# The start of a fused causal-convolution and GELU-MLP kernel: block 0's tokens in order, block 1's x issued earlier, W_in chunks in another order, and taps of the convolution joined

## The chip, the cores and the metric

The kernel runs on one core of a Trainium2 chip. The core has five engines with separate instruction streams: PE (TensorE, matrix products into PSUM), DVE (VectorE), ACT (ScalarE), POOL (GpSimd) and SP (SyncE, which here only issues DMAs). They meet at semaphores. ACT and POOL issue some DMAs too, and all DMAs are carried out by the same 16 DMA engines. The metric is the device time of one execution in microseconds (us), as the median over runs; smaller is better.

## The reference, cut to what matters

x has 8 sequences of 4096 tokens with 192 features; 8 heads of 24 features share 7 convolution weights each. The weights go through a softmax over the taps, the convolution is causal along the sequence, and its result goes through a two-layer MLP with exact GELU.

```python
w = np.exp(weight - np.max(weight, axis=-1, keepdims=True))
w = w / (np.sum(w, axis=-1, keepdims=True) + 1e-09)            # [8 heads, 7 taps]
x_pad = np.concatenate([np.zeros((B, 6, D)), x], axis=1)
idx = np.arange(S)[:, None] + np.arange(7)[None, :]
x_unf = x_pad[:, idx, :].reshape(B, S, 7, 8, 24)
conv = np.einsum('hk,bskhg->bshg', w, x_unf).reshape(B * S, 192)
h = conv @ w_in                                                # [32768, 2048]
g = 0.5 * h * (1.0 + erf(h / sqrt(2)))
out = g @ w_out                                                # [32768, 192]
```

## The kernel before, in words

**Layout.** The 32768 tokens are cut into two halves of 16384. A block takes the same stretch of tokens from both halves: the first six blocks (0 to 5) have 256 tokens of each half, the others 512. Half 0 lies in partitions 0 to 63 and half 1 in partitions 64 to 127. The 192 features are three planes (p = 0, 1, 2) of 64, feature 3j+p in plane p, row j of a half.

**Load (`load`, L319).** x of a block comes in four DMAs, one for each half and each half of the features (q), in fp32, 32 tokens side by side in the partitions, into one of three buffers `xin`. For block 0 each partition takes eight neighbouring tokens in one piece of 1440 floats (5760 bytes, of which the other feature half is not used); for the other blocks each token's half row is a piece of its own, 96 floats (384 bytes). So block 0's tokens sit in another order than those of the other blocks, and its halo, its taps' offsets (32 columns per tap) and its stores follow that order.

**Convolution.** DVE transposes `xin` into `xT` (`trans`, L518; three calls, one for each plane). For blocks 0 and 1 the convolution is done by PE: the planes are cast to bf16 into `xTb` (ACT for block 0, POOL for block 1), PE multiplies by seven diagonal matrices `dg` (`pconv`, L700) into the four PSUM banks `ob`, and ACT and DVE copy the result to `xc` (`conv_out`, L182). For blocks from 2 on DVE does it (`conv`, L538): for each tap k and each plane p one call, the first a multiplication (L555), the other six a multiply-add onto `acc` (L562), the last of them writing `xc` in bf16. For blocks 4, 5 and 6 ACT does tap 0 (`first_tap`, L652). POOL copies the six columns of halo between blocks (`halo`, L408).

**The two products.** `mm1` (L737) multiplies `xc` by `win` into `hp`, two buffers of two banks; one slice i holds two chunks of 128 hidden features for a block of 256 tokens and one chunk for a block of 512. ACT does the GELU from `hp` into `gT` (L684). `mm2` (L793) and for the long blocks `mm2_t` (L823) multiply by `wout` into `ob`. The product with W_out of block n-1 is cut into units that are put between the slices of block n, so PE's order is written out by hand: slice, units, slice, units. DVE and ACT bring `ob` to `osb`, and SP stores it.

**W_in and W_out.** W_in comes by three pairs of POOL DMAs (pieces of 256, 256 and 512 columns); each half of the partitions loads only its own 1024 columns, and DVE copies each piece across to the other half (`dup`, L501). `CH` (L87) is the order in which a half uses its 16 chunks. W_out comes in fp32 by four SP DMAs and POOL casts it (`S_WOG` counts the casts).

**Order at the start.** Each engine runs its list in order. SP: weights, half of block 0's x, a wait for the first piece of W_in (L873), block 1's x, four DMAs of W_out, x of blocks 2 and 3, and then loads and stores in turn. DVE: softmax, the diagonals `dg`, `trans(0)`, two `conv_out` of block 0, `dup(0)`, `dup(1)`, `trans(1)`, `dup(2)`, `conv_out` of block 1, block 2. PE: 16 matmuls on zeros (L698), `pconv` of block 0, slices of block 0, with `pconv` of block 1 behind slices 4 and 5 (`behind`, L732), and so on. A slice waits until the GELU two slices before has emptied its `hp` buffer.

Of the kernel before, what the change touches and what calls it, by code (L numbers as in the profile page):

```python
# [11 lines left out]
def bass_lightweight_conv__then__act_gelu_exact_kernel(  # L12
# [36 lines left out]
    HX = 8  # L49
# [3 lines left out]
    HL = 32 * HB  # L53
    XB = HL + WS[0]
# [32 lines left out]
    CH = [[(8 * hf + i) % NF for i in range(NF)] for hf in range(2)]  # L87
# [3 lines left out]
    for n in range(NB):  # L91
        k = 64 if n == 0 or M0 <= n < M1 else 16 * NG[n] if n < NB - 1 else 32 * NG[n]
        OUTS.append(k * (NG[0] if n == 0 else 1) + (OUTS[n - 2] if n >= 2 else 0))
# [15 lines left out]
    with es:  # L109
# [94 lines left out]
        NCV = NP * KS  # L204
# [6 lines left out]
        def cast(e, n, p):  # L211
            e.wait_ge(S_TR, NP * n + p + 1)
            e.tensor_copy(
                ap(xTb[PC[n]], p * XB + HX, [[NP * XB, 128], [1, WS[n]]]),
                ap(xT[n % 2], p * XW + HX, [[NP * XW, 128], [1, WS[n]]]),
            ).then_inc(S_CAST[PC[n]])

        def cvd(n):

            return sum(NCV - NP * (m in K0) for m in range(n + 1) if m not in PC)  # L220


        HC = [0]
        for n in range(NB):
            HC.append(HC[n] + (1 + NP if n == 0 else 1))
# [93 lines left out]
        def load(e, n, qs=(0, 2, 1, 3), sm=None):  # L319
            mb = WS[n] // 32  # L320
            if n >= NX:
                e.wait_ge(S_TR, NP * (n - NX + 1))
            for q in qs:
                off = ((q // 2) * HALF + OFF[n]) * D + DQ * (q % 2)
                if n == 0:

                    dst = [[TB // 32 * DQ, 32], [1, mb * D - DQ]]
                    src = [[mb * D, 32], [1, mb * D - DQ]]
                else:
                    dst = [[TB // 32 * DQ, 32], [DQ, mb], [1, DQ]]  # L330
                    src = [[D, 32], [32 * D, mb], [1, DQ]]
                e.dma_start(  # L332
                    ap(xin[n % NX], 32 * q * (TB // 32 * DQ), dst), ap(xt, off, src)
                ).then_inc(sm or S_XIN[n % NX], 16)

        def store(e, m):
            if m < M0:
                for g in range(NG[m]):
                    wait_ev(e, m, g)
                    if m > 0:  # L340

                        e.dma_start(
                            ap(
                                outt,
                                (OFF[m] + 128 * g) * C,
                                [[C, 128], [HALF * C, 2], [1, C]],
                            ),
                            ap(osb[m % 2], g * C, [[8 * C, 128], [4 * C, 2], [1, C]]),
                        ).then_inc(S_OUT[m % 2], 16)
                        continue  # L350
                    mb = WS[m] // 32
                    for q in range(4):

                        e.dma_start(
                            ap(
                                outt,
                                (OFF[m] + 4 * g + q) * C,
                                [[mb * C, 32], [HALF * C, 2], [1, C]],
                            ),
                            ap(  # L360
                                osb[m % 2],
                                32 * q * 8 * C + g * C,
                                [[8 * C, 32], [4 * C, 2], [1, C]],
                            ),
                        ).then_inc(S_OUT[m % 2], 16)
# [18 lines left out]
        def _(g):  # L384
# [23 lines left out]
            def halo(n):  # L408
                if n == 0:

                    t = xTb[0]
                    g.memset(
                        ap(t, 0, [[NP * XB, 128], [XB, NP], [32, HB]]), 0.0
                    ).then_inc(S_HALO)
                    for p in range(NP):
                        g.wait_ge(S_TR, p + 1)
                        g.tensor_copy(
                            ap(t, p * XB + 1, [[NP * XB, 128], [32, HB], [1, 31]]),
                            ap(
                                xT[0],  # L420
                                p * XW + HX + WS[0] - HL,
                                [[NP * XW, 128], [32, HB], [1, 31]],
                            ),
                        ).then_inc(S_HALO)
                    return

                t, tw = (xTb[1], XB) if n in PC else (xT[n % 2], XW)
                dst = ap(t, HF, [[NP * tw, 128], [tw, NP], [1, HB]])
                if n >= 2:
                    if n - 2 in PC:  # L430
                        wait_pc(g, n - 2, NP - 1)
                    else:
                        g.wait_ge(S_CV, cvd(n - 2))
# [3 lines left out]
                g.wait_ge(S_TR, NP * n)  # L437
                if n == 1:
                    src = ap(
                        xT[0],  # L440
                        HX + WS[0] - HL + 31,
                        [[NP * XW, 128], [XW, NP], [32, HB]],
                    )
                else:
                    src = ap(
                        xT[(n - 1) % 2],
                        HF + WS[n - 1],
                        [[NP * XW, 128], [XW, NP], [1, HB]],
                    )
# [469 lines left out]
```

## Time and profile before

| | us |
|---|---|
| median of 4 runs (lowest, highest) | 682.68 (682.41, 683.15) |
| the profiled execution: its time | 683.15 |
| its span, first to last instruction | 681.4 |
| PE busy | 674.9 |
| DVE busy | 561.1 |
| ACT busy | 536.6 |
| POOL busy | 38.9 |

The profiled execution's time is 1.7 us above its span: that part lies outside the instructions. The profile names an engine, a line of the kernel, what is written and read (`xc<-xT,wcol,acc` reads xT, wcol and acc), how often it occurs, and its busy time. The chain of waits is followed back from the last instruction to what released each step. SPq and POOLq are the queues in which an engine issues DMAs.

### The profile page before, as it was taken

The page shows a single profiled execution, that of the slowest core. Times are in us where ns is not written, and L with a number is a line of the kernel's source. Part 1 is how long each engine was busy: PE and PEld are TensorE (multiplying, and loading weights), DVE is VectorE, ACT ScalarE, POOL GpSimd, SP SyncE. Part 2 cuts the span into 40 slices and gives each one's busy share as a digit, 9 for nine tenths or more (in the row PEclk, how much of TensorE's full clock was granted, in tenths as well). Part 3 has the DMA queues.
Part 4 walks back from the last instruction along what each step waited for, and adds up shares of the span by engine and source line. Part 5 has one row for each costly group of instructions (what it writes and reads, how often), then busy time and mean ns, then how long its engine had stood idle before and what let it go on. Part 6 is the DMA issues. An engine that isn't in the chain of part 4 may idle for free.

```text
span 681.4 us, 27316 instructions
## 1 busy us (share of the span) xinstructions
PE 674.9 (99%) x12576; PEld 410.7 (60%) x12576; DVE 561.1 (82%) x906; ACT 536.6 (79%) x548; POOL 38.9 (6%) x57
## 2 busy tenths in 40 slices
PE   8999999999999999999999999999999999999998
PEld 4899755555555555555555555555555555555557
DVE  6899989888889888898888898888898888988611
ACT  6899988777787777787877788777778777778772
POOL 5125100000000000000000000000000000000000
PEclk9999999999999999999999999999999999999999
DMA  9345332234442244432244422344322444321123
GB/s 225 83 101 130 72 71 72 44 77 95 96 93 54 45 94 94 95 78 49 66 94 95 94 64 47 82 94 96 94 49 50 95 94 96 74 45 26 48 50 94
DMA packets 132994, 54.79 MB, mean 80 GB/s; under 512 B 126480, under 2 KB 132752, under 8 KB 132880
## 3 DMA queue, kind: packets, MB, share of 16 engines
q1 hardware_dynamic: 130960, 51.50, 32.5%
q8 instruction: 98, 1.61, 1.0%
q0 software_dynamic: 1248, 0.79, 0.8%
q10 hardware_dynamic: 672, 0.76, 0.4%
q14 instruction: 16, 0.13, 0.1%
HBM read 28.66 MB, written 25.17 MB: 79 GB/s over the span
## 4 chain that ended last, share of the span: by engine, by line
PE 95%; DMA 2%; DVE 1%; SPq 1%; issue 0%; POOL 0%; POOLq 0%
PE hp L763 47%; PE ob L823 43%; PE ob L793 5%; DMA xin<-in_x_dram 1%; DVE acc L562 1%; PE hp L793 1%; DMA win<-in_moe_w_in_dram 1%; SPq L332 1%; SPq L877 0%; DVE xT L529 0%; POOL win L387 0%; DVE acc L555 0%; DVE xc L562 0%; DVE osb L283 0%; POOLq L904 0%
## 5 line engine op out<-in xcount | busy, mean ns | idle before, releaser
L684 ACT ACTIVATE gT<-hp 128x1024 bf16<-128x1024 f32 x512 | 523.2, 1024 | 129.6 <-PE hp L763 126.4
L763 PE MATMUL hp<-xc,win 64*64 64x512 bf16 (+2 forms) x6048 | 419.3, 366 | 2.4 <-ACT gT L684 1.1
L823 PE MATMUL ob<-gT,wout 64*64 64x512 bf16 x5376 | 366.3, 376 | 0.0
L562 DVE SCALAR_TENSOR_TENSOR acc<-xT,wcol,acc 128x512 f32<-128x512 f32 (+1 forms) x495 | 314.5, 700 | 0.0
L763 PEld LDWEIGHTS hp<-xc,win 64*64 64x64 bf16 (+1 forms) x6048 | 189.9, 106 | 135.3 <-ACT gT L684 3.5
L823 PEld LDWEIGHTS ob<-gT,wout 64*64 64x64 bf16 x5376 | 172.1, 118 | 122.9
L314 DVE STREAM_TRANSPOSE osb<-ob 128x512 f32<-128x512 f32 x84 | 74.1, 885 | 99.9 <-PE ob L823 99.9
L529 DVE STREAM_TRANSPOSE xT<-xin 128x512 f32<-128x512 f32 (+1 forms) x105 | 78.6, 799 | 4.0 <-DMA xin<-in_x_dram 4.0
L562 DVE SCALAR_TENSOR_TENSOR xc<-xT,wcol,acc 128x512 bf16<-128x512 f32 (+1 forms) x99 | 65.2, 715 | 0.0
L450 POOL COPY xT<-xT 128x18 f32<-128x18 f32 x30 | 27.9, 930 | 505.0 <-DVE xT L529 482.6
L793 PE MATMUL ob<-wout,gT 64*128 64x192 bf16 x896 | 47.6, 243 | 0.0
L793 PEld LDWEIGHTS ob<-wout,gT 64*128 64x128 bf16 x896 | 40.1, 94 | 3.9 <-issue 0.4
L555 DVE TENSOR_SCALAR acc<-xT,wcol 128x512 f32<-128x512 f32 (+1 forms) x90 | 37.6, 474 | 1.1
L698 PE MATMUL hp<-warm 128*128 128x512 bf16 x16 | 6.0, 555 | 1.3 <-DVE warm L466 1.3
L285 ACT ACTIVATE osb<-ob 128x192 f32<-128x192 f32 x2 | 0.7, 331 | 7.1 <-PE ob L793 7.1
L793 PE MATMUL hp<-wout,gT 64*128 64x192 bf16 x128 | 5.9, 243 | 0.0
L283 DVE COPY osb<-ob 128x192 f32<-128x192 f32 x2 | 0.7, 358 | 6.1 <-PE ob L793 6.1
L793 PEld LDWEIGHTS hp<-wout,gT 64*128 64x128 bf16 x128 | 5.3, 94 | 0.0
L657 ACT ACTIVATE acc<-xT,wcol 128x256 f32<-128x256 f32 (+1 forms) x9 | 5.2, 575 | 0.0
L698 PEld LDWEIGHTS hp<-warm 128*128 128x128 bf16 x16 | 2.1, 135 | 4.6 <-issue 3.0
L270 ACT ACTIVATE osb<-ob 128x384 f32<-128x384 f32 x10 | 4.9, 486 | 0.0
L193 DVE CAST xc<-ob 64x256 bf16<-64x256 f32 (+3 forms) x8 | 2.8, 357 | 1.5 <-PE ob L714 1.4
(36 smaller groups left out, 31.4 us busy)
## 6 DMA issues: line engine op xcount, KB each, us to landing
out_dram<-osb SPq DMA_DIRECT2D x122, 192.0 KB, 3.1
xin<-in_x_dram SPq DMA_DIRECT2D x116, 192.0 KB, 4.1
xin<-in_x_dram SPq DMA_DIRECT2D x20, 96.0 KB, 3.5
woutf<-in_moe_w_out_dram SPq DMA_DIRECT2D x4, 384.0 KB, 7.0
win<-in_moe_w_in_dram POOLq DMA_DIRECT2D x4, 96.0 KB, 4.3
win<-in_moe_w_in_dram POOLq DMA_DIRECT2D x2, 192.0 KB, 4.7
out_dram<-osb SPq DMA_DIRECT2D x8, 48.0 KB, 2.0
out_dram<-osb ACTq DMA_DIRECT2D x4, 96.0 KB, 2.0
```

Source lines behind the costliest of these rows:

```text
L314: v.transpose(ap(osb[m % 2], j, [[8 * C, 128], [C // 2, TB // 32], [NP, 32]]), bank(ring(m, j)),).then_inc(S_EV)
L332: e.dma_start(ap(xin[n % NX], 32 * q * (TB // 32 * DQ), dst), ap(xt, off, src)).then_inc(sm or S_XIN[n % NX], 16)
L450: g.tensor_copy(dst, src).then_inc(S_HALO)
L529: v.transpose(ap(xT[n % 2], p * XW + HX, [[NP * XW, 128], [1, w]]), ap(xin[n % NX], p, [[TB // 32 * DQ, 128], [D if n == 0 else DQ, w // 3 ...
L555: ins = v.tensor_scalar(a, src, wk, None, ALU.mult)
L562: ins = v.scalar_tensor_tensor(dst, src, wk, a, op0=ALU.mult, op1=ALU.add)
L657: a.activation(out=acc[n % 2][:, p * TB : p * TB + w], in_=ap(xT[n % 2], p * XW + HX, [[NP * XW, 128], [1, w]]), func=AF.Copy, scale=wcol[ ...
L684: a.activation(out=ap(gT[n % 2], i * c * 2 * w, dst), in_=ap(hp[u % 2], 0, src), func=AF.Gelu,).then_inc(S_GELU)
L698: t.matmul(hp[1][:, 0:512], warm[:, 0:128], warm[:, :])
L763: ins = t.matmul(hp[u % 2][fo : fo + fw, o : o + w], ap(win, f1, [[NP * F, 64], [2, fw]]), xc[n % 2][r, p * TB : p * TB + w], start=(p == ...
L793: ins = t.matmul(bb[sub], gT[m % 2][r, c0 : c0 + 128], wout[r, CH[sub][i] * C : (CH[sub][i] + 1) * C], start=(ph == 0 and i == 0), stop=(p ...
L823: ins = t.matmul(bank(ring(m, j), slice(64 * h, 64 * h + 64), w), ap(wout, 64 * hf * NF * C + CH[h][i] * C + j, [[NF * C, 64], [NP, 64]],) ...
```

## The change

The diff has these parts.

1. Block 0's x is loaded like the others': half rows of 96 floats, tokens in order. Its halo becomes a zeroed strip (one memset on DVE instead of a memset and three copies on POOL), its taps' offsets go by one column, and its stores become two DMAs instead of eight.
2. SP waits for block 0's x instead of the first piece of W_in before it issues block 1's x.
3. `CH` lets both halves use chunks 8 to 11 of the other half (copied by `dup(0)` and `dup(1)`) in slices 2 and 3 of block 0, ahead of the third piece of W_in (slices 4 and 5) and its copy (slices 6 and 7). The waits in `mm1` follow this order, and the wait for the last two casts of W_out moves from unit 4 to unit 8.
4. `pconv` of block 1: taps 6, 5, 4 of its first two products go behind slice 3 instead of slice 4.
5. From block 2 on, `trans` is one call for the three planes, and `conv` two calls per tap: planes 0 and 1 together, and plane 2. The list of DVE's work (`plan`, `side`) is renumbered for that, and `mm1` starts a block when planes 0 and 1 of `xc` are there and waits for plane 2 before its product.
6. The matmuls on zeros at the start are 12 instead of 16.

```diff
-    HL = 32 * HB
-    XB = HL + WS[0]
+    XB = HX + WS[0]
...
-    CH = [[(8 * hf + i) % NF for i in range(NF)] for hf in range(2)]
+    CH = [[(8 * hf + 8 * (i // 4 % 2) + 4 * (i // 8) + i % 4) % NF for i in range(NF)] for hf in range(2)]
...
+            if n == 0:
+                ins = e.activation(out=dst, in_=src, func=AF.Copy)
+            else:
+                ins = e.tensor_copy(dst, src)
...
+        def trd(n):
+            return NP * (n + 1) if n < 2 else 2 * NP + n - 1
...
-                if n == 0:
-                    dst = [[TB // 32 * DQ, 32], [1, mb * D - DQ]]
-                    src = [[mb * D, 32], [1, mb * D - DQ]]
-                else:
-                    dst = [[TB // 32 * DQ, 32], [DQ, mb], [1, DQ]]
-                    src = [[D, 32], [32 * D, mb], [1, DQ]]
+                dst = [[TB // 32 * DQ, 32], [DQ, mb], [1, DQ]]
+                src = [[D, 32], [32 * D, mb], [1, DQ]]
...
+            v.memset(ap(xTb[0], HF, [[NP * XB, 128], [XB, NP], [1, HB]]), 0.0).then_inc(S_HALO)
...
+                if n in PC:
+                    out = ap(xT[n], p * XW + HX, [[NP * XW, 128], [1, w]])
+                    src = ap(
+                        xin[n % NX], p, [[TB // 32 * DQ, 128], [DQ, w // 32], [NP, 32]]
+                    )
+                else:
+                    out = ap(xT[n % 2], HX, [[NP * XW, 128], [XW, NP], [1, w]])
+                    src = ap(
+                        xin[n % NX],
+                        0,
+                        [[TB // 32 * DQ, 128], [1, NP], [DQ, w // 32], [NP, 32]],
+                    )
+                v.transpose(out, src).then_inc(S_TR)
...
+            def conv(n, k, s):
+                p0, pn = (0, 2) if s == 0 else (2, 1)
...
+                src = ap(xT[n % 2], p0 * XW + HF + kt, [[NP * XW, 128], [XW, pn], [1, w]])
+                a = ap(acc[n % 2], p0 * TB, [[NP * TB, 128], [TB, pn], [1, w]])
...
-                    ops[9:9] = [("t", n + 1, p) for p in range(NP)]
+                    ops[6:6] = [("t", n + 1, 0)]
...
-                for j, at in enumerate([(n + 2, 18), (n + 3, 6), (n + 3, 9)]):
+                for j, at in enumerate([(n + 2, 12), (n + 3, 4), (n + 3, 6)]):
...
-                a.wait_ge(S_TR, NP * n + p + 1)
+                a.wait_ge(S_TR, trd(n))
...
-            for i in range(16):
+            for i in range(12):
...
-                (0, 4): [(1, kd, k) for k in taps for kd in (0, 1)],
+                (0, 3): [(1, kd, k) for k in taps if k > 3 for kd in (0, 1)],
+                (0, 4): [(1, kd, k) for k in taps if k <= 3 for kd in (0, 1)],
...
-                        t.wait_ge(S_CV, cvd(n))
-                if n == 0 and i < 3:
-                    t.wait_ge(S_WIN[i], 32)
-                if n == 0 and 4 <= i < 7:
-                    t.wait_ge(S_DUPE, 2 * (i - 4) + 2)
+                        t.wait_ge(S_CV, cvd(n) - 1)
+                if n == 0 and i in (0, 1, 4):
+                    t.wait_ge(S_WIN[i if i < 2 else 2], 32)
+                if n == 0 and i in (2, 3, 6):
+                    t.wait_ge(S_DUPE, 2 * (i - 2) + 2 if i < 4 else 6)
...
-                        if n == 1 and un in ((0, 0, 0), (0, 0, 4)):
-                            t.wait_ge(S_WOG, 2 + un[2] // 2)
+                        if n == 1 and un in ((0, 0, 0), (0, 0, 8)):
+                            t.wait_ge(S_WOG, 2 + un[2] // 4)
...
             load(sp, 0, (0, 1))
-            sp.wait_ge(S_WIN[0], 32)
+            sp.wait_ge(S_XIN[0], 64)
             load(sp, 1)
```

## The prediction

> **What bounds the kernel now.** I read the page first, then the chain of waits over the first 30 us in order of time, then the timeline of the same stretch, then the groups with their shapes kept apart.
>
> The page, its span, its busy times and its chain:
>
> ```profile
> span 681.4 us, 27316 instructions
> PE 674.9 (99%) x12576; PEld 410.7 (60%) x12576; DVE 561.1 (82%) x906; ACT 536.6 (79%) x548; POOL 38.9 (6%) x57
> PE 95%; DMA 2%; DVE 1%; SPq 1%; issue 0%; POOL 0%; POOLq 0%
> ```
>
> PE holds 95% of the chain. Taken singly from the trace, PE's matmuls after 29.70 us never start more than 0.26 us apart, except once by 0.31 us at 667.5. So the 651.7 us from there to the end are PE's own work. The change leaves that work's matmuls alone, so its worth is the time by which block 2's first slice (29.70) moves, plus any new gap after it. The chain before it:
>
> ```profile
> 2.10 4.77 DMA win<-in_moe_w_in_dram
> 6.88 0.33 SPq L332
> 8.74 0.46 SPq L877
> 13.19 6.96 DMA xin<-in_x_dram
> 20.17 1.36 DVE xT L529 x3
> 22.43 4.82 DVE acc L562 x13
> 29.07 0.49 DVE xc L562
> 29.70 0.38 PE hp L763 x3
> ```
>
> SP sits behind W_in's first piece until 6.88, so x of blocks 1 and 2 and W_out come late; block 2's convolution runs from 20.17 to 29.6 and PE waits for it. The timeline shows a second chain just below it:
>
> ```profile
> 5.50 0.15 PEld L698 LDWEIGHTS hp<-warm 128*128 128x128 bf16 x1 [0.28 <-issue]
> 5.93 0.79 PEld L698 LDWEIGHTS hp<-warm 128*128 128x128 bf16 x4 [0.28 <-issue]
> 6.04 1.35 DVE L529 STREAM_TRANSPOSE xT<-xin 128x256 f32<-128x256 f32 x3 [0.19 <-DMA xin<-in_x_dram]
> 11.93 1.35 DVE L529 STREAM_TRANSPOSE xT<-xin 128x256 f32<-128x256 f32 x3 [0.96 <-DMA xin<-in_x_dram]
> 15.78 1.02 ACT L684 ACTIVATE gT<-hp 128x1024 bf16<-128x1024 f32 x1 [0.63 <-PE hp L763]
> 17.06 3.96 ACT L684 ACTIVATE gT<-hp 128x1024 bf16<-128x1024 f32 x4 [0.26 <-PE hp L763]
> 18.14 0.83 PE L763 MATMUL hp<-xc,win 64*128 64x256 bf16 x12 [0.45 <-ACT gT L684]
> 29.70 0.83 PE L763 MATMUL hp<-xc,win 64*128 64x256 bf16 x12 [0.86 <-DVE xc L562]
> ```
>
> Block 0 is paced by the GELUs (single starts 10.22, 11.15, 12.18, 13.10, 14.13: 0.976 apart). They break for 0.63 and 0.26 us because PE stands at block 1's convolution, whose casts come late because x of block 1 does. Block 1's first slice waits for a GELU (18.14); from there PE runs unbroken, its last mm2 matmul starting at 28.60.
>
> **The change, part by part.**
>
> *Block 0's x.* Four DMAs of 180 KB become four of 96 KB. The DMA view of 1.5 to 5.2 us gives ACT's queue 96 packets, 0.37 MB and 39.7% of 16 engines: 15.7 bytes/ns per engine. The page's SP queue, nearly all 384-byte pieces, moves 51.50 MB in 32.5% of 16 x 681.4 us: 14.5 bytes/ns. So 0.74 MB cost the 16 engines 2.9 us now and 0.39 MB will cost 1.7. Landing lies between 5.2 us (last issue 1.63 plus the 3.5 us median of 96 KB loads) and 6.3 (4.4, plus 0.3 for sharing): I take under 5.85, nearest to the median row. There `dg` ends (5.23+0.62), so `trans(0)` gains 0.17 at most, which I take; the other end is -0.3. The Trainium skill, "DMA: Bandwidth & Descriptors", Specifications, speaks against it: below 512 bytes a transfer misses line rate. Read as half rate, 0.39 MB would cost as much as 0.79 MB, above today's 0.74: no 0.17 and a total of 681.4. The two rates per byte above do not agree with that, so they decide.
> POOL's memset and three copies go, off the path (done by 7.80 beside ACT's casts to 7.84); DVE's memset falls into its 1.47 us wait for the weights. Six fewer store issues at 0.43 us free SP by 2.6 us after 27 us, which delays nothing.
>
> *Block 1's x.* Its four issues, W_out's four and x of block 2 move up on SP from 6.88 to block 0's landing: 4.7 to 6.0 us, I take 5.2. Moved past the W_in wait, its pieces share the DMA engines with W_in, on POOL's queue until 9.7. The work is 1.2 us less than before, so x of block 1 lands between 10.1 (last issue 6.6 plus 3.5) and 11.9 (as now). DVE reaches `trans(1)` at 10.97-0.17 = 10.8. I take 10.8, nearer the row of 96 KB loads. W_in's third piece is delayed by at most block 1's 1.7 us, to 11.4; slice 4 needs it at 13.1.
>
> *Chunk order and waits.* Slices 2 and 3 now wait for `dup(0)` and `dup(1)`, done at 9.9 and 10.8; their GELU waits end at 11.1 and 12.0. Slice 6 needs `dup(2)`, done by 13.6, at 15.7. W_out's first two casts end at 16.7 today, its last at 19.5; the units need them at 18.4 and 19.7. All hidden; uncovered, they would each cost what they are late. The four matmuls on zeros end before `pconv` starts: nothing.
>
> *Block 1's convolution.* With `trans(1)` at 10.8, casts of planes 0 and 1 end at 11.8 and 12.25 (1.0 and 1.4 later today). Slice 3 starts at 12.07, its last matmul at 12.64; 12 pconv matmuls at 0.0256 (28 in 0.69) and 0.2 us of change of tile on either side bring slice 4 to 13.11, where its GELU buffer frees as well. Slice 4 to GELU is 0.87: 13.98, no break. Then 16 pconv matmuls: slice 5 at 14.46, GELU 15.33. Then 28 more (0.37): slice 6 at 15.74, GELU 16.61 instead of 17.06. Block 1's first slice waits for its end: 17.70 instead of 18.14, and 28.60 becomes 28.15. Block 2 can start at 28.24.
>
> *Joined taps.* The groups by shape, of which these carry it:
>
> ```profile
> L562 DVE SCALAR_TENSOR_TENSOR acc<-xT,wcol,acc 128x512 f32<-128x512 f32 x435 | 290.2, 730 | 0.0
> L562 DVE SCALAR_TENSOR_TENSOR acc<-xT,wcol,acc 128x256 f32<-128x256 f32 x60 | 24.3, 485 | 0.0
> L529 DVE STREAM_TRANSPOSE xT<-xin 128x512 f32<-128x512 f32 x87 | 70.5, 861 | 0.0
> ```
>
> Busy time per call: 667 ns at 512 columns, 405 at 256. So a column costs 1.02 ns and a call 143 ns. Two joined planes of 256 are 512 columns: 0.67 us; bounds are 0.67 and twice 0.405. Block 2: transpose 1.16 (768 columns; 0.45 at 256, 0.81 at 512), tap 0 0.72, six taps of 1.07: 8.3 us, planes 0 and 1 after 7.9, against 9.4 from 20.17 to PE's start. With x landing between 18.0 and 20.17 (I take 19.1: the 1.2 us of DMA work) `xc` is ready at 27.0, at worst at 28.2, or at 29.0 if joining also saved nothing. PE comes at 28.24: I take the wait of 0.86 as gone (the far end keeps 0.8 of it), and what is late next is PE itself.
>
> In long blocks 143 ns x 9 is 1.3 us of DVE per 20.72 us block: worth nothing, since DVE already idles 2.9 us per block for PE (the wait of L314). The renumbered evacuations come at most one 1.19 us call later; the second half-pass of mm2_t needs its bank 4.3 us after it is freed today.
>
> *A wait added.* ACT's `first_tap` of block 4 waits for all three planes, not the first. It sits before slice 3's GELU of block 2: 34.12-1.46 = 32.66. DVE ends that transpose 13.4 us after x of block 2: 32.5, at worst 33.6. Behind it are GELUs with some 0.75 us of slack, so PE loses 0 to 0.2; I take 0.
>
> Sum: 29.70 to 28.24, **1.46 us less**, 0.44 from block 1 and 1.02 from block 2's wait with its restart. In the profiled execution 683.15 becomes 681.69; it stands 0.47 above the median of 682.68, so the median becomes **681.2**.
>
> **The rivals.**
>
> *R1: x of block 1 lands no earlier* (11.9), since W_in shares the engines. Slice 4 then stands at plane 1's cast (13.35): slice 4 at 13.9, GELU 6 at 17.40, block 1 at 18.5, block 2 at 29.04: 0.65 less, 682.0. For it: the DMA engines are busy 90% or more from 2.5 us on. Against: 1.2 us less work and a free SP.
>
> *R2: the GELUs never break*, with pconv in their shadow: GELU 6 at 15.95, block 1 at 17.05, 2.1 us less, 680.6. Against it: PE's time between GELU releases is 0.98, a slice takes 0.76 with its change, and the pconv pieces 0.41 and 0.37.
>
> *R3, slower: the joined calls cost more than their halves.* DVE's 2.9 us of idle per long block cover seven calls up to 1.33+0.42 = 1.75 us each; beyond that every block pays. At 2.0 us, some 1.7 us x 25 blocks: 725. For it: no multiply-add over two planes is in the trace. Against: the row's cost goes by columns, and `win`'s copy over three planes (64x768, 420 ns) shows no penalty.
>
> *R4, the other slow end: PE's clock.* Weight loads of the zero matmuls are 0.43 us apart until 5.93 and about 0.21 after: full clock comes after 4.7 us of work. Twelve end near 6.2, only just past it. If the clock came 3.4 us later, the pconv (1.5) and the first slices (1.1) would run at half: 2.6-1.5 = 1.1 slower, 683.8; it decides from 1.5. The Trainium skill, "TensorE: Matmul & The Clock Gate", Part 1, says that the gate looks at free-running windows of some 3.4 us; by it a window ending after 6.4 would hold the 0.7 us hole before pconv. That window is still some 80% busy, and here the grant came at 5.9.
>
> **How the numbers follow.** Forecast 0.60 (681.2, its own range 680.8 to 681.8), R1 0.20, R2 0.08, R3 0.07, R4 0.05. A measurement tells about 0.2%, 1.37 us, from no change: under 681.3 is faster. The forecast sits 0.1 inside, 0.70 of it: 0.42, with R2 0.50. Same: 0.18 and R1, 0.38. Slower: R3 and R4, 0.12. The range leaves out R3 and R4 and takes R2 less 0.2 and R1 plus 0.5: 680.4 to 682.5.
>
> **What would show it.** SP issues block 1's x near 5; `trans(1)` follows `dup(1)` without a DMA wait; block 1's first slice is at 17.7 and block 2's at 28.2 with no wait for `xc`; joined multiply-adds take 1.2 us at 1024 columns; 651.7 us follow. Wrong: a DMA wait at `trans(1)`, a clock grant after 7 us, PE gaps after 30 us.

## The result, and the profile after

The changed kernel takes **684.19 us** (median of 34 runs, 682.84 to 686.52) against **682.89 us** (median of 56 runs, 682.02 to 684.15) of the kernel before. The ratio is **1.0022 [1.0017, 1.0027]**: slower by 0.22%, where 681.2 was forecast, faster. Both the direction and the range were wrong.

To understand the number, one thing is needed: the executions of the changed kernel fall into two groups by the granted TensorE clock. With the profiled one there are 35 of them; 19 had a mean clock of 1.000 and a median of 683.52 (682.84 to 684.37), 15 had 0.998 and 685.27 (684.62 to 685.87), and one had 0.995 and 686.52. The times of the kernel before show no such groups. So two things are to be explained: some 0.6 us (683.52 against 682.89) in the undisturbed executions, and 1.75 us more in nearly half of them. The profiled execution (683.46 us, span 681.7, clock 1.000) is of the first kind.

The page after, span, busy times and engines of the chain:

```profile
span 681.7 us, 27003 instructions
PE 674.3 (99%) x12572; PEld 408.8 (60%) x12572; DVE 528.5 (78%) x613; ACT 536.6 (79%) x548; POOL 30.0 (4%) x53
PE 97%; DMA 1%; SPq 0%; ACT 0%; DVE 0%; POOL 0%; issue 0%
```

DVE lost 32.6 us of work (561.1 before) and the span grew by 0.3: PE is the bound throughout, as it was. The chain of waits over the first 20 us tells where it now begins (start in us, length, what):

```profile
1.64 3.40 DMA xin<-in_x_dram
5.06 0.31 SPq L329
...
6.40 6.70 DMA xin<-in_x_dram
...
13.12 0.53 DVE xT L491
...
13.70 0.81 POOL xTb L217 x2
...
14.55 0.52 PE ob L666 x10
15.07 0.76 PE hp L719 x12
...
18.48 1.03 ACT gT L636
...
19.56 0.83 PE hp L719 x12
```

The chain no longer passes through block 2's convolution; it passes through **x of block 1**. SP issues that load at 5.06, 1.8 us earlier than before (6.88), but it lands at 13.10, 6.7 us after its last issue, where in the profile of before it landed at 11.91, 3.7 us after its last issue. (Two kernels below whose x and W_in are loaded as before have it at 13.09 and 12.90, so the issue brought x no earlier; that it made x later by 1.2 us isn't shown.) What follows is a straight line: `trans(1)` at 13.12, the casts of two planes on POOL, `pconv` of block 1, and the GELU that block 1's first slice (19.56) waits for. The waits between 8 and 30 us (us in total, times, the longest) give the price:

```profile
ACT gT L636 <- PE hp L719: 5.6, 9, 2.6
DVE xT L491 <- DMA xin<-in_x_dram: 4.2, 2, 3.0
PEld ob L666 <- POOL xTb L217: 2.5, 2, 2.2
```

DVE waits 3.0 us for x of block 1, PE's weight loads 2.2 us for the casts, and a GELU 2.6 us for PE. Taken singly from the trace, PE's matmuls have one gap of 2.22 us from 11.94, between slice 3 and `pconv`. Side by side, with the profiled execution of each kernel:

| | before | forecast | after |
|---|---|---|---|
| `trans(0)` starts | 6.04 | 5.87 | 5.22 |
| block 0's first slice | 9.01 | 8.84 | 8.16 |
| x of block 1 issued | 6.88 | 5.2 | 5.06 |
| `trans(1)` starts | 11.93 | 10.8 | 13.12 |
| block 1's first slice | 18.14 | 17.70 | 19.56 |
| x of block 2 there, its transpose starts | 20.17 | 19.1 | 20.01 |
| block 2's first slice | 29.70 | 28.24 | 30.09 |
| from there to the end of the span | 651.7 | 651.7 | 651.6 |

Block 0 starts 0.85 us earlier; 2.27 us are then lost up to block 1's first slice, of which the wait for block 2's `xc` (0.86 before, gone now) and the matmuls after it give 1.03 back. The difference at block 2, +0.39, is but for 0.08 us the difference of the spans (0.31).

### The profile page after: what moved, and what is told of

Read it like the earlier page. It is cut to its first block, busy times and chain, and to the rows that moved or that the text cites. A ratio compares the mean times of both kernels' runs of the same rounds, so it can differ in the third digit from the quotient of the medians.

```text
span 681.7 us, 27003 instructions
## 1 busy us (share of the span) xinstructions
PE 674.3 (99%) x12572; PEld 408.8 (60%) x12572; DVE 528.5 (78%) x613; ACT 536.6 (79%) x548; POOL 30.0 (4%) x53
## 3 DMA queue, kind: packets, MB, share of 16 engines
q1 hardware_dynamic: 131312, 51.33, 32.6%
## 4 chain that ended last, share of the span: by engine, by line
PE 97%; DMA 1%; SPq 0%; ACT 0%; DVE 0%; POOL 0%; issue 0%
PE hp L719 48%; PE ob L779 43%; PE ob L749 5%; DMA xin<-in_x_dram 1%; PE hp L749 1%; PE ob L666 0%; SPq L329 0%; ACT gT L636 0%; POOL xTb L217 0%; DVE xT L491 0%; SPq L827 0%; DVE osb L285 0%
## 5 line engine op out<-in xcount | busy, mean ns | idle before, releaser
L636 ACT ACTIVATE gT<-hp 128x1024 bf16<-128x1024 f32 x512 | 523.1, 1024 | 130.8 <-PE hp L719 127.7
L519 DVE SCALAR_TENSOR_TENSOR acc<-xT,wcol,acc 128x1024 f32<-128x1024 f32 (+1 forms) x330 | 295.7, 948 | 4.1 <-ACT acc L609 3.8
L719 PEld LDWEIGHTS hp<-xc,win 64*64 64x64 bf16 (+1 forms) x6048 | 188.0, 106 | 135.2 <-ACT gT L636 2.0
L316 DVE STREAM_TRANSPOSE osb<-ob 128x512 f32<-128x512 f32 x84 | 74.0, 884 | 129.4 <-PE ob L779 129.4
L491 DVE STREAM_TRANSPOSE xT<-xin 128x1536 f32<-128x1536 f32 (+2 forms) x39 | 74.5, 1919 | 4.2 <-DMA xin<-in_x_dram 4.2
L519 DVE SCALAR_TENSOR_TENSOR xc<-xT,wcol,acc 128x1024 bf16<-128x1024 f32 (+1 forms) x66 | 60.5, 954 | 0.0
L400 POOL COPY xT<-xT 128x18 f32<-128x18 f32 x30 | 20.1, 669 | 512.6 <-DVE xT L491 486.1
L749 PEld LDWEIGHTS ob<-wout,gT 64*128 64x128 bf16 x896 | 38.6, 94 | 5.1 <-issue 0.4
L512 DVE TENSOR_SCALAR acc<-xT,wcol 128x512 f32<-128x512 f32 (+2 forms) x60 | 33.7, 604 | 1.1
L666 PE MATMUL ob<-xTb,dg 64*64 64x256 bf16 (+1 forms) x112 | 3.7, 247 | 2.0 <-POOL xTb L217 1.9
L666 PEld LDWEIGHTS ob<-xTb,dg 64*64 64x64 bf16 x112 | 2.6, 106 | 3.6 <-POOL xTb L217 2.5
```

What stands on the lines that cost most here:

```text
L316: v.transpose(ap(osb[m % 2], j, [[8 * C, 128], [C // 2, TB // 32], [NP, 32]]), bank(ring(m, j)),).then_inc(S_EV)
L400: g.tensor_copy(dst, src).then_inc(S_HALO)
L491: v.transpose(out, src).then_inc(S_TR)
L512: ins = v.tensor_scalar(a, src, wk, None, ALU.mult)
L519: ins = v.scalar_tensor_tensor(dst, src, wk, a, op0=ALU.mult, op1=ALU.add)
L636: a.activation(out=ap(gT[n % 2], i * c * 2 * w, dst), in_=ap(hp[u % 2], 0, src), func=AF.Gelu,).then_inc(S_GELU)
```

## Experiments

Every kernel below computes the whole reference. Each comparison is with the kernel before on the same chip. The kernels fall into three questions: what takes the clock away, why x of block 1 comes late, and what the other parts are worth.

### What takes the clock away

The nearest suspect was the forecast's own rival R4, the four zeros that were taken away. Two kernels put that to the test from both sides, and two more shorten the standstill of PE instead.

**The changed kernel with 16 zeros:**

```diff
-            for i in range(12):
+            for i in range(16):
```

> The changed kernel with 16 matmuls on zeros instead of 12, nothing else. Two theories on the 15 of 34 executions whose granted clock is 0.998 and whose time is 1.7 us above the others: (C) the shorter warm-up lets PE's clock come late, (S) the standstill of 2.2 us before block 1's convolution lets the clock drop again. By C all executions show a clock of 1.000 and the median is 683.4 to 683.7, that of the undisturbed group. By S the two groups stay, median 684 to 685.

Measured: 685.55 us (684.90 to 686.63, 5 runs), ratio 1.0041 [1.0028, 1.0054], against 682.84. All five executions had the lower clock (0.998 in four, 0.995 in one). More zeros didn't bring the clock back, so the warm-up falls as the cause. The trace of this kernel shows the loss itself. The columns of the windows view are the stretch, its length, the busy time of PE, PEld, DVE, ACT and POOL (with the number of instructions), the granted clock, the DMA share and GB/s:

```profile
5.30:12.10 6.80, 5.67 (x105) 3.52 (x104) 3.66 (x9) 4.69 (x10) 0.72 (x2) 1.00 1.02 176
12.10:15.50 3.40, 1.26 (x24) 0.65 (x18) 1.76 (x4) 1.66 (x2) 1.21 (x3) 1.00 1.06 346
15.50:18.90 3.40, 3.40 (x44) 1.98 (x40) 2.30 (x4) 1.02 (x1) 1.97 (x4) 0.50 1.22 212
```

The clock is granted in full at 5.29, is cut to one half from 15.53 to 18.94, and is full again. 10.24 us of full clock are three times 3.413, and the cut lasts 3.41. PE was busy for 37% (1.26 of 3.40 us) of the window just before the cut, because PE stood there from 12.7 on. In the profiled execution of the changed kernel itself, which kept its clock (full from 6.05), windows of the same length divide the same hole between them:

```profile
9.47:12.88 3.41, 2.19 (x34) 1.24 (x30) 0.63 (x2) 3.40 (x4) 0.00 (x0) 1.00 1.09 253
12.88:16.29 3.41, 2.03 (x40) 1.22 (x40) 3.10 (x5) 0.81 (x2) 2.59 (x5) 1.00 1.10 336
```

The emptier of the two has 60% (2.03 of 3.41), and the clock stayed. The Trainium skill, "TensorE: Matmul & The Clock Gate", Part 1, gives a free-running window of 4096 cycles at 1.2 GHz, 3413 ns; the rows agree with its length. The page speaks of an idle window as what takes the clock away; here a window with PE 37% busy was enough, and the measurement decides.

**The kernel before with 12 zeros:**

```diff
-            for i in range(16):
+            for i in range(12):
```

> The kernel before with 12 matmuls on zeros instead of 16, nothing else; it has no standstill of PE over 0.8 us. By C about half of the executions have a clock of 0.998 and are some 1.7 us longer: the median goes from 682.9 to anywhere between 683 and 684.5, and the spread upwards reaches 684.5 or more. By S nothing changes: 682.7 to 683.1 and all at 1.000.

Measured: 682.75 us (682.22 to 684.88, 12 runs), ratio 1.0000 [0.9992, 1.0008], the clock 1.000 in all twelve. Part 6 costs nothing and R4 is out.

**The changed kernel with 16 zeros and block 1's convolution where it was before** (part 4 undone):

```diff
-                (0, 3): [(1, kd, k) for k in taps if k > 3 for kd in (0, 1)],
-                (0, 4): [(1, kd, k) for k in taps if k <= 3 for kd in (0, 1)],
+                (0, 4): [(1, kd, k) for k in taps for kd in (0, 1)],
```

> The changed kernel with 16 matmuls on zeros and with block 1's convolution behind slices 4 and 5 again, as before. Theory D: block 1's x lands at 13.1 because its pieces alternate with W_in's on the DMA engines, and PE, which has the convolution one slice earlier now, stands for its casts with slice 4 behind it. By D x lands where it does (13.1), slice 4 and its GELU run before the standstill, block 1's first slice moves from 19.6 to 18.6 or 18.7, and the time falls by about 0.9 against the same with the new order: 682.5 to 682.8. By the rival P (PE's order hides nothing, since the GELU stream is broken by the late convolution either way) the time is that of the new order, 683.5.

Measured: 683.19 us (682.40 to 684.24, 11 runs), ratio 1.0004 [0.9996, 1.0013], the clock 1.000 in all eleven. In its profiled execution PE waits 1.1 us for the casts (2.0 in the kernel with 16 zeros and part 4), and slice 4 lies ahead of that wait. The same x, just as late (13.70 and 13.69), with a shorter standstill: the clock stays, and the time falls by 2.36 us. That is more than the 0.9 expected; what is above it goes with the clock, which the expectation left out. So the standstill, not the number of zeros, decides about the clock.

**The changed kernel with part 4 alone undone**, with its 12 zeros:

```diff
-                (0, 3): [(1, kd, k) for k in taps if k > 3 for kd in (0, 1)],
-                (0, 4): [(1, kd, k) for k in taps if k <= 3 for kd in (0, 1)],
+                (0, 4): [(1, kd, k) for k in taps for kd in (0, 1)],
```

> The changed kernel with part 4 alone undone: block 1's convolution stands behind slices 4 and 5 as before, 12 zeros. Theory: x of block 1 still lands near 13.1, but slice 4 no longer queues behind its casts, so PE stands some 1.4 us instead of 2.2, block 1's first slice is 0.3 us earlier (near 18.5-19.3) and the clock is full in all runs: 683.0 (682.6 to 683.5), ratio 1.000. If part 4 costs nothing: 684.2 with the lower clock in about half of the runs, ratio 1.002.

Measured: 683.41 us (681.90 to 685.72, 12 runs), ratio 1.0011 [1.0002, 1.002], against 682.82. The time is in the expected range, but the clock wasn't full in all: two of twelve had 0.998 (684.66 and 685.72). Part 4 thus accounts for some 0.8 us of the loss against the 684.19 of the whole change, more than half of it by the clock (the executions at 1.000 alone have medians of 683.2 and 683.5); without it the standstill (1.4 us of waiting for the casts in this profiled execution) takes the clock away less often, but not never.

### Why x of block 1 comes late

Theory D, after the first runs: x of block 1 is late because its small pieces take turns with W_in's on the DMA engines. It predicts that an x issued still earlier, ahead of most of W_in, comes in time, and that an x issued somewhat later, as before, isn't helped at all.

**16 zeros, and x of block 1 issued right behind block 0's,** with a wait ahead of W_out instead:

```diff
-            sp.wait_ge(S_XIN[0], 64)
             load(sp, 1)
+            sp.wait_ge(S_WIN[1], 32)
```

> The changed kernel with 16 matmuls on zeros; SP issues block 1's x right behind block 0's, with no wait, and waits for W_in's second piece before it issues W_out. By D x of block 1 is then ahead of most of W_in's pieces and lands by 7 to 8, trans(1) has no DMA wait and starts at 10.1, block 1's first slice comes at 16.9 to 17.5 and block 2's at 27.4 to 28.0 if its x is there: 2.0 to 2.7 less than the changed kernel undisturbed, 680.8 to 681.5. Cost that could eat it: W_in's first piece, needed at 8.2, is delayed by up to 1.6. By the rival H (half rows of 384 bytes are slow to land whatever they meet) x lands after 10 all the same and the time stays within 0.5 of 683.5.

Measured: 681.87 us (681.63 to 682.38, 11 runs), ratio 0.9987 [0.9979, 0.9996], the clock 1.000 in all. The chain of waits of this kernel runs through x of block 0 alone:

```profile
1.64 4.23 DMA xin<-in_x_dram
...
12.05 0.83 PE hp L719 x12
12.88 0.45 PE ob L666 x12
13.33 0.76 PE hp L719 x12
14.10 0.56 PE ob L666 x16
14.66 0.76 PE hp L719 x12
15.42 0.52 PE ob L666 x28
...
17.82 0.83 PE hp L719 x12
```

Slices and `pconv` of block 1 alternate without a hole, with part 4 in place. `trans(1)` starts at 10.84, right behind `dup(1)`, and block 1's first slice at 17.82; the forecast had 10.8 and 17.70. So the working of the forecast holds from `trans(1)` on, if x is there and `trans(0)` starts where it was taken (5.89 here, 5.87 in the forecast). The median is 0.4 above the expected 681.5, as `trans(1)` is 0.7 later than the 10.1 expected; x itself landed at 8.20. That W_out is issued later in this kernel isn't what brings x in time: in the last kernel of this section W_out has no wait, and x landed at 8.43.

**The same edit with the 12 zeros of the changed kernel:**

```diff
-            sp.wait_ge(S_XIN[0], 64)
             load(sp, 1)
+            sp.wait_ge(S_WIN[1], 32)
```

> The changed kernel with one edit: SP issues block 1's x right behind block 0's and waits for W_in's second piece before W_out (12 matmuls on zeros stay). Theory D+S: the whole loss of the change lies in block 1's x meeting W_in, and in the clock that the standstill drops. By D+S there is no standstill, the clock is 1.000 in all executions and the median is that with 16 zeros, 681.7 to 682.1. Theory C in what is left of it (12 zeros are too few by themselves): some executions at 0.998 and 683 or more.

Measured: 681.64 us (681.10 to 682.31, 11 runs), ratio 0.9980 [0.9971, 0.9989] against 683.12, the clock 1.000 in all. One line of SP's order makes the whole change faster than the kernel before, by 0.2%, and takes both losses away; it is 2.5 us faster than the changed kernel. What is left in its profiled execution is one new wait: W_out is issued only at 8.41, and PE stands for its casts, with a gap of 0.88 us from one matmul to the next at 19.03 and one of 0.30 at 34.98.

```profile
PE ob L749 <- POOL wout L409: 0.6, 1, 0.6
```

**The changed kernel with SP's old wait** (part 2 undone):

```diff
-            sp.wait_ge(S_XIN[0], 64)
+            sp.wait_ge(S_WIN[0], 32)
             load(sp, 1)
```

> The changed kernel with SP's old wait, for W_in's first piece, before block 1's x; all else as changed. By D the wait hardly matters by itself: with block 0's x at 0.39 MB W_in's first piece lands near 5.0 to 5.5 too, x of block 1 is issued within 0.5 of where it is now and meets the second and third piece of W_in, the standstill before its convolution stays between 1.5 and 2.5 and the time between 683 and 685, with part of the executions at 0.998. By the rival E (the early issue is the harm) x lands near 12, the standstill shrinks to under 0.8 and the time falls to 682 or below.

Measured: 683.70 us (683.05 to 685.59, 11 runs), ratio 1.0019 [1.0010, 1.0029] against 683.12; the clock 0.998 in five (685.02 to 685.59) and 1.000 in six (683.05 to 683.70). Issuing x of block 1 0.9 us later changes nothing: it was issued at 5.98 and landed at 13.14. Rival E, that part 2 itself made x late, falls: with x of block 0 in half rows W_in's first piece is through at 5.96 already, so the old wait also ends while W_in is under way. This kernel's profiled execution lost its clock, and its windows give the second point for it:

```profile
8.12:11.53 3.41, 2.60 (x46) 1.64 (x40) 2.27 (x6) 2.65 (x5) 0.00 (x0) 1.00 1.02 185
11.53:14.94 3.41, 1.62 (x28) 0.86 (x24) 1.74 (x4) 2.12 (x3) 1.19 (x3) 1.00 1.07 354
14.94:18.35 3.41, 3.41 (x44) 1.88 (x40) 2.26 (x4) 1.02 (x1) 2.67 (x4) 0.50 1.21 251
```

A window with 48% (1.62 of 3.41) was followed by the cut. In the profile with part 4 alone undone, the window from 12.79 to 16.21 had 56% (1.92 of 3.42) and kept the clock. Between 48% and 56% lies the limit, as PE's modelled busy time shows it.

The full clock came at anything from 4.69 to 7.12 us in the profiles, so the windows fall on the hole in different places. How empty a window can be at most is found by sliding a stretch of 3.41 us over the trace of each profiled execution, from 7 to 30 us. It orders the kernels nearly as the cuts do:

| kernel | PE busy in the emptiest stretch | executions with a cut |
|---|---|---|
| changed, 16 zeros | 35% | 5 of 5 |
| changed | 37% | 16 of 35 |
| changed, SP's old wait | 48% | 5 of 11 |
| changed, part 4 undone | 48% | 2 of 12 |
| before, 12 zeros | 55% | 0 of 12 |
| changed, x of block 1 first and no wait ahead of W_out | 56% | 0 of 11 |
| changed, 16 zeros, part 4 undone | 57% | 0 of 11 |
| changed, x of block 1 first (with 12 and 16 zeros) | 68% and 74% | 0 of 11 each |

How the two queues share the engines is seen in the DMA view of 5 to 11 us, of the changed kernel and of the kernel before. q0 is POOL's queue (W_in), q1 is SP's (x and W_out). The changed kernel:

```profile
DMA packets 1727, 0.95 MB, mean 158 GB/s; under 512 B 933, under 2 KB 1727, under 8 KB 1727
q0 software_dynamic: 832, 0.59, 77.0%
q1 hardware_dynamic: 895, 0.36, 28.2%
```

The kernel before:

```profile
DMA packets 2322, 1.20 MB, mean 200 GB/s; under 512 B 1181, under 2 KB 2322, under 8 KB 2322
q0 software_dynamic: 1210, 0.77, 92.9%
q1 hardware_dynamic: 1112, 0.43, 33.3%
```

In the same 6 us the engines are nearly as full but move 21% less. Counted in the trace, from 8 to 9.5 us each half microsecond of the changed kernel holds 46 to 55 of W_in's pieces of 1024 bytes and 77 to 88 of x's of 384; the kernel before moves 97 W_in pieces in the half microsecond from 8.0, with no x beside them, and then up to 383 x pieces from 9.5, with only six of W_in. So the two queues share the engines: beside one piece of W_in go 1.5 to 1.9 of x's, and x, which has small pieces, gets the smaller part of the bytes. In this execution of the kernel before, x came last but almost alone.

Sharing with x is not all that slows W_in: with SP's old wait, W_in moves only 48 to 65 pieces in each half microsecond from 7.0 to 9.0, with at most 16 of x beside them, against 97 and 98 from 8.0 to 9.0 before. What else slows it isn't shown.

Nor was x almost alone in every execution of the old order. Read from the trace of each kernel, in us:

| kernel | block 1's x first issued | landed | W_in's last piece landed |
|---|---|---|---|
| before | 6.88 | 11.91 | 10.10 |
| before, 12 zeros | 6.59 | 13.09 | 11.56 |
| before, joined taps alone (below) | 6.70 | 12.90 | 11.02 |
| before with parts 1 and 5 (below) | 5.85 | 12.81 | 10.88 |
| changed, SP's old wait | 5.98 | 13.14 | 11.46 |
| changed | 5.06 | 13.10 | 11.93 |
| changed, part 4 undone | 4.76 | 13.60 | 12.29 |
| changed, 16 zeros; the same, part 4 undone | 5.45; 5.16 | 13.69; 13.70 | 11.84; 12.52 |
| the four with block 1's x right behind block 0's | 2.12 to 2.14 | 8.19 to 8.43 | 10.51 to 14.52 |

Issued anywhere from 4.76 to 6.88, x lands 1.2 to 1.9 us after W_in's last piece, between 12.81 and 13.70 in all but one profile. The profile of before, from which the forecast was made, is the exception. What the change loses against the old order in an undisturbed execution is therefore better read against the kernel before with 12 zeros, whose x is as late: there slice 4 starts at 13.64 and block 1's first slice at 18.68, in the changed kernel at 15.00 and 19.56, since `pconv` now stands ahead of slice 4 (with part 4 undone slice 4 starts at 12.43). The 0.88 us are there at block 2's first slice too (29.21 and 30.09), and the medians differ by 0.77 (682.75 and 683.52).

**W_out earlier.** Two kernels, after the one with x of block 1 first, vary SP's wait ahead of W_out. With the wait for W_in's first piece:

```diff
-            sp.wait_ge(S_XIN[0], 64)
             load(sp, 1)
+            sp.wait_ge(S_WIN[0], 32)
```

> The changed kernel with block 1's x issued right behind block 0's, and SP waiting for W_in's first piece (not its second) before W_out. Theory: W_out is issued near 7 instead of 8.4, its last casts end before unit 8 and x of block 2 lands about 1 us earlier, so the stands of 0.88 us at 19.0 and 0.30 us at 35.0 go: 680.6 (680.3 to 681.2), ratio 0.9965. Rival: W_out's pieces take turns with W_in's second and third piece, which then come late for slices 1 and 4: 681.6 or more, ratio 0.998 or above.

Measured: 681.61 us (681.25 to 682.55, 11 runs), ratio 0.9984 [0.9975, 0.9992] against 682.82. In its profiled execution W_out is issued at 6.75, and the stands of 0.88 and 0.30 us are gone: from block 1's first slice (17.86) PE has no gap over 0.26 us but the one near the end that all have. The time is that of the kernel with the later wait all the same, so the expected microsecond is missing. The time is the rival's (681.6 or more), but its lateness of W_in for slices 1 and 4 isn't in the trace: neither waits for it. In this execution x of block 0 came 0.73 us later (`trans(0)` at 5.93 instead of 5.20); whether that happens in most executions, or the stand for W_out is smaller in most executions of the other kernel, isn't settled by one profile each.

With no wait at all ahead of W_out:

```diff
-            sp.wait_ge(S_XIN[0], 64)
             load(sp, 1)
```

> As the kernel with the wait for the first piece, but with no wait ahead of W_out at all (issued near 4.5, right behind block 1's x). Theory that pieces of all queues take turns: W_in's second and third pieces are delayed by 1 to 3 us, slice 1 or slice 4 stands for them, block 1's first slice comes 0.5 to 2 us later than 17.8 and the clock may fall: 682.0 to 684.5, ratio 0.999 to 1.002. Rival, that only the early pieces matter: 680.6, ratio 0.9965.

Measured: 683.11 us (682.73 to 683.63, 11 runs), ratio 1.0004 [0.9995, 1.0012], the clock 1.000 in all. Now it is W_in that shares the engines, with W_out. Its chain of waits and its waits from 8 to 30 us:

```profile
5.20 9.32 DMA win<-in_moe_w_in_dram
14.52 0.14 issue
14.65 0.83 PE hp L719 x12
```

```profile
DVE win L455 <- DMA win<-in_moe_w_in_dram: 3.1, 2, 1.9
PE hp L719 <- DMA win<-in_moe_w_in_dram: 1.9, 2, 1.0
```

W_in's third piece lands at 14.52, 9.3 us after its issue (5.9 us was the median of the two such loads in the changed kernel), and slice 4 waits for it, as slice 1 does for the second piece. Against the kernel with the wait for the first piece 1.5 us are lost (683.11 against 681.61), all that had been saved. This is theory D's mechanism with the roles exchanged: an early issue isn't a priority here, it is a claim on a share.

### What the other parts are worth

**The kernel before with the joined taps alone** (part 5):

```diff
-            def conv(n, k, p):
+            def conv(n, k, s):
+                p0, pn = (0, 2) if s == 0 else (2, 1)
...
-                        t.wait_ge(S_CV, cvd(n))
+                        t.wait_ge(S_CV, cvd(n) - 1)
```

> The kernel before with the joined taps alone (part 5). My price: block 2's convolution takes 1.4 less, so the wait of 0.86 and its restart before block 2's first slice (1.02 together) go and nothing else changes: 681.8 to 682.1, all at a clock of 1.000. By the rival J (joined calls buy nothing, since block 2's x or PE decides) 682.7 to 683.0.

Measured: 682.42 us (682.12 to 683.88, 11 runs), ratio 0.9996 [0.9987, 1.0005] against 683.12; the median is 0.70 lower, which can't be told from no change, and above the 681.8 to 682.1 expected. In its profiled execution PE doesn't wait for block 2's `xc`. But neither does it with the old taps in the kernel before with 12 zeros, where x of block 2 was transposed from 19.61 and PE came to block 2 at 29.21: the wait of 0.86 that was to go stood in the one profile of before, not in every execution. The chain of waits of the execution with the joined taps shows something else at its start, the 16 zeros themselves. Its timeline has the late x of block 1, under the old order of loads:

```profile
1.26 6.51 PE hp L710 x16
7.76 0.90 PE ob L726 x27
```

```profile
6.70 1.81 SPq L335 DMA_DIRECT2D xin<-in_x_dram  x4
12.92 1.35 DVE L546 STREAM_TRANSPOSE xT<-xin 128x256 f32<-128x256 f32 x3 [1.61 <-DMA xin<-in_x_dram]
```

The full clock came only at 7.12 in that execution, so the 16 zeros lasted to 7.7 and held the convolution of block 0 back. The zeros cost nothing only where the clock comes in time.

**The kernel before with parts 1 and 5** (block 0's x in half rows, joined taps; SP's order, chunk order, block 1's convolution and 16 zeros as before). Against the kernel before:

```diff
-                if n == 0:
-                    dst = [[TB // 32 * DQ, 32], [1, mb * D - DQ]]
-                    src = [[mb * D, 32], [1, mb * D - DQ]]
-                else:
-                    dst = [[TB // 32 * DQ, 32], [DQ, mb], [1, DQ]]
-                    src = [[D, 32], [32 * D, mb], [1, DQ]]
+                dst = [[TB // 32 * DQ, 32], [DQ, mb], [1, DQ]]
+                src = [[D, 32], [32 * D, mb], [1, DQ]]
...
+            def conv(n, k, s):
+                p0, pn = (0, 2) if s == 0 else (2, 1)
```

> The kernel before with the half rows in order (part 1) and the joined taps (part 5) only: SP's wait for W_in's first piece, the old chunk order, block 1's convolution behind slices 4 and 5, 16 zeros. Against the kernel before with the joined taps alone it shows what part 1 does. By D x of block 1 still meets W_in and lands at 12.5 to 13.5, and W_in's third piece, which the old order needs in slice 2, comes late too: block 1's first slice at 18.3 to 19.3, time 682.3 to 683.5. If half rows only helped (0.8 of earlier start), it would be at 681.2.

Measured: 682.84 us (682.32 to 684.29, 11 runs), ratio 1.0002 [0.9993, 1.0011], the clock 1.000 in all. In its chain, W_in's first piece ends at 5.83, where it ended at 6.68 with the joined taps alone; x of block 1 is thereby issued at 5.85, meets W_in's later pieces, and lands at 12.81:

```profile
5.85 0.31 SPq L329
...
7.19 5.62 DMA xin<-in_x_dram
...
18.40 0.83 PE hp L718 x12
```

The half rows move SP's issue forward by 0.85 us against the kernel with the joined taps alone (6.70), and x lands where it landed there (12.90). So part 1 alone brings block 1's x no earlier either. Block 1's first slice is at 18.40 against 18.69, and the medians, 682.84 and 682.42, show no gain from part 1; the 681.2 of the rival, in which half rows only help, falls.

## Why the prediction was wrong, point by point

**What bounds the kernel.** Right: PE's 651.7 us from block 2's first slice held (651.6), no gaps appeared after 30 us, and DVE idles more (129.4 us before the transposes of `ob`, L316, against 99.9 before).

**Block 0's x.** Right in sign, mis-sized: `trans(0)` gained 0.82, not 0.17. The cap was the end of `dg` at 5.85 in the one profiled execution of before, and that was an odd one: the weights were there at 2.78 in it, and at 2.15 to 2.22 in eleven of the other twelve profiles here, two kernels with block 0's x in long pieces among them. With `dg` done near 5.25, x decides: `trans(0)` starts at 5.82 and 5.94 in those two, and at 5.16 to 5.61 in the six with half rows whose next load isn't right behind. The half rows are worth 0.2 to 0.8 us, where the rule on 512 bytes, read as half rate, would have given nothing.

**Block 1's x: the step that failed.** "x of block 1 lands between 10.1 (last issue 6.6 plus 3.5) and 11.9 (as now)", with 10.8 taken for `trans(1)`. It landed at 13.10, beyond the far bound, and `trans(1)` waited 3.0 us for it, which was the forecast's own first sign of being wrong. The sum of the bytes was right (1.2 us less work), but the reasoning from it was not: less work in all says nothing about one transfer when two queues share the engines. The 3.5 us median of such loads was measured where x ran almost alone, and was taken over to a place with W_in beside it. The far bound failed too, because "as now" was one execution: in the two profiles with the old loads x landed at 13.09 and 12.90. R1 named this cause with 0.20, but priced it with the same bound, 682.0. The forecast of an earlier landing fails with it for x of block 2: 20.01 against 19.1.

**Block 1's convolution.** The arithmetic was right given its input: with x in time, block 1's first slice is at 17.82 against the 17.70 worked out. With x late, part 4 turns against the kernel, since slice 4 now queues behind `pconv` of block 1 on PE. The forecast gave this under R1 a slice 4 at 13.9 and a total still below before; it was 15.0.

**PE's clock.** R4 looked at the clock at the start, where nothing happened: 12 zeros in the kernel before, ratio 1.0000. That a standstill of some 2 us could take the clock away again, in about half of the executions, was in none of the cases. It makes the difference between 683.52 and the median of 684.19. That R4's 683.8 lies near the result is chance.

**Joined taps.** Right: block 2's transpose to its `xc` took 8.3 us (20.01 to 28.32), as worked out. Calls over 1024 columns took 1.28 us instead of 1.2, those over 512 columns 0.72 instead of 0.67; R3 falls.

```profile
L519 DVE SCALAR_TENSOR_TENSOR acc<-xT,wcol,acc 128x1024 f32<-128x1024 f32 x145 | 185.1, 1276 | 0.0
L519 DVE SCALAR_TENSOR_TENSOR acc<-xT,wcol,acc 128x512 f32<-128x512 f32 x165 | 118.3, 717 | 3.4 <-ACT acc L609 3.2 <-DVE acc L512 0.3
```

The wait for `xc` went, but PE came later than before, so the 1.02 us priced for it bought nothing in this kernel. Alone the joined taps show 0.70 by the medians, within the noise; the wait that they were to remove isn't there in the kernel before with 12 zeros.

**Chunk order, zeros, the added wait of `first_tap`.** The zeros cost nothing (measured alone). The chunk order was not tried alone; no wait for `dup` or for W_out's casts stands on PE after 12 us in the profiled execution. What it can save is seen in the kernel before with 12 zeros, where slice 2 waits 1.1 us for W_in's third piece:

```profile
5.20 6.36 DMA win<-in_moe_w_in_dram
11.56 0.14 issue
11.69 0.85 PE hp L763 x12
```

In the changed kernel this piece landed at 11.93, and no slice waits for it. The taps on ACT held DVE for 3.8 us in all, small beside DVE's idle time.

## What to carry to other kernels

A load issued earlier doesn't land earlier by that alone: here issues from 4.76 to 6.70 us all landed between 12.81 and 13.70, behind the stream they were put into. Price such a load by who shares the DMA engines in that stretch, not by the total of bytes, and ask whether it can be put ahead of the stream instead. When work that waits for such a load is moved forward on an in-order engine, ask what queues behind it if the load is late; here that turned a wait of 3.0 us for x into a gap of 2.2 us between PE's matmuls, and the gap into a clock loss. Durations and caps taken from one profiled execution should be checked against a second one where the forecast leans on a small difference: x at 11.9, `dg` at 5.85 and the wait for `xc` were all of one execution.

## What the runs showed of the hardware that was not expected

- The clock is judged in stretches of 3.413 us, and not only at the start: a stretch with PE busy for 37% or 48% was followed by one at half clock, those with 56% and 60% were not. A cut cost 1.75 us, about half of 3.41. With 12 zeros it hit 16 of 35 executions of the changed kernel. That the stretches fall differently on the same hole fits the profiles, but only one execution of each kernel was profiled. Why it hit all of the five with 16 zeros wasn't settled.
- A load of four 96 KB parts landed 3.7 us after its last issue when almost alone, and 4.8 to 7.5 us after it in the eight profiles in which it was issued into more of W_in's stream; in the changed kernel the engines then moved 158 instead of 200 GB/s over 6 us.
- A single landing of a small load can be late by 0.6 us (the weights at 2.78 instead of 2.15 to 2.22), and the full clock came anywhere from 4.69 to 7.12 us.
